# Decoding 64-bit weights through PSUM: the scaled high words move from an SBUF tile into the banks of the first MoE's output

## Chip, core and metric

One core of a Trainium2 chip runs the whole program. The metric is device time in microseconds (us): the time before is the median of three runs, 1158.89 us (1158.51 to 1161.87).

## What is computed

Attention with a top-32 mask over 4 x 8 heads of 576 tokens, then a dense feed-forward layer ("the first MoE", 2304 tokens, 512 to 2048 to 512, softplus between), then a layer of 8 experts with one expert per token. In short:

```
scores = scale * np.matmul(q, k.transpose(0, 1, 3, 2))
kth = np.partition(scores, -top_k, axis=-1)[..., -top_k:-top_k + 1]
attn = softmax(np.where(scores >= kth, scores, -1e9))
x = attn @ v            # as 2304 x 512
h = x @ w_in
x = (np.maximum(h, 0.0) + np.log1p(np.exp(-np.abs(h)))) @ w_out
...
h = np.maximum(xe @ w1[e], 0.0)
out[mask] = gate_w[mask, None] * (h @ w2[e])
```

`moe_w_in` and `moe_w_out` arrive as 64-bit floats, 8 bytes an element, and the kernel makes 32-bit floats of them itself. That decode is what the change touches.

## The kernel before

The program has two parts. Part one does attention, the decode and the first MoE, interleaved; part two does the experts.

**Attention** goes in 72 groups of two tiles of 128 query rows. For a group TensorE computes the scores (L365) into one PSUM tile, ScalarE copies them to SBUF (L373), VectorE finds the 32 largest of each row with maxima and replacements (L401 to L425) and makes the mask (L433 or L436), GpSimd applies the mask and splits the result into two 16-bit halves (L437, L442, L443), a DMA transposes them (L445), and three groups later TensorE multiplies with v (L460, L462). There is one PSUM tile for the scores, so the scores of the next group wait until VectorE has read it last, at L417.

**The decode** (`decode`, L196) takes 32 blocks of 128 x 512 weights: 16 of `w_in`, 16 of `w_out`, two ahead of the first group and then four behind each group in the program's text. For a block SyncE loads the 64-bit words (L198) into one of two tiles `w`; ScalarE scales the high word down (L204) into the SBUF tile `xr`; VectorE shifts that left by 3 bits, in place (L206), and joins it with the sign bit of the high word (L209), in place again; ScalarE scales the low word (L208), in place; GpSimd adds both as integers (L210). The tile `xr` has two buffers. A buffer is held from L204 until L210 has read it.

**The first MoE** goes in units of two tiles of 128 tokens, each of 16 steps (one per 128 columns of the hidden layer), 160 steps in all. A step has layer 1 (12 matmuls into `h`, L547; activations L551 to L555 on ScalarE; a sum into `g` on GpSimd, L556) and, two steps later, layer 2 (`layer2`, L570): one matmul per tile of tokens (L581, or L578 for the last units) that adds to the unit's two output tiles `y`. The pool `ps_y` of those tiles has two buffers, a PSUM bank each; `g` has four. Layer 1 can therefore run a few steps ahead of layer 2, and then has to wait for it.

**The order.** The order of instructions on each engine is fixed when the program is built: a list scheduler takes the program's text with priorities (attention ahead of decode and MoE) and its own estimate of times. Each engine then works through its list and waits at the front. A pool gives its buffers out in the order of the program's text: a tile that is asked for waits until the tile that held the buffer has been read last. In that text all 32 decodes stand ahead of the first unit's first layer-2 step.

```python
ps_y = pool("ps_y", 2, space=PSUM)
x2p = pool("x2p", X2B)
u.y = [ps_y.tile([128, DM], F32, name="y") for _ in u.tiles]
```

Of the kernel before, what the change touches and what calls it, by code (L numbers as in the profile page):

```python
# [8 lines left out]
F32 = mybir.dt.float32  # L9
F32R = mybir.dt.float32r  # L10
F16 = mybir.dt.float16
I32 = mybir.dt.int32
U32 = mybir.dt.uint32
AF = mybir.ActivationFunctionType
ALU = mybir.AluOpType
# [5 lines left out]
NT, DM, DFF = 2304, 512, 2048  # L21
# [11 lines left out]
ROWW = DM + 1  # L33
# [25 lines left out]
C = 512  # L59
# [103 lines left out]
def part_one(tc, ctx, q, k, v, w_in, w_out, const, ident, before, ones, iota_e, reg_e, wg,  # L163
             ohcum, done, early, table, rows, flags, sums, w_sums):
    nc = tc.nc
    late = []

    def pool(name, bufs, **kw):
        return ctx.enter_context(tc.tile_pool(name=name, bufs=bufs, **kw))
# [12 lines left out]
    x2p = pool("x2p", X2B)  # L182
# [3 lines left out]
    ps_y = pool("ps_y", 2, space=PSUM)  # L186
# [9 lines left out]
    def decode(src, kk, c0, dst):  # L196
        w = dec.tile([128, 2 * C], I32, name="w", bufs=DWB)
        nc.sync.dma_start(w, src[:, kk, 2 * c0:2 * (c0 + C)])  # L198
        w = w.rearrange("p (a b) -> p a b", b=2)
        hi, lo = w[:, :, 1], w[:, :, 0]  # L200
        a = x2p.tile([128, ROWW], F32, name="xr")[:, :C]


        nc.scalar.activation(a, hi.bitcast(F32), AF.Copy, scale=2.0 ** -111)  # L204
        u = a.bitcast(U32)
        nc.vector.tensor_scalar(u, u, 3, None, op0=ALU.logical_shift_left)  # L206

        nc.scalar.activation(lo, lo.bitcast(U32), AF.Copy, scale=2.0 ** -29)  # L208
        nc.vector.scalar_tensor_tensor(u, hi.bitcast(U32), 0x80000000, u, op0=ALU.bitwise_and, op1=ALU.bitwise_or)  # L209
        nc.gpsimd.tensor_tensor(out=dst.bitcast(I32), in0=a.bitcast(I32), in1=lo, op=ALU.add)  # L210

    def decode_w_in(kk, j):
        t = dec.tile([128, C], F32, name="t")
        decode(w_in_v, kk, j * C, t)
        nc.scalar.activation(w_in_s[:, kk, j, 1], t, AF.Abs, accum_out=w_sums[:, j, kk:kk + 1])
        nc.scalar.activation(w_in_s[:, kk, j, 0], t, AF.Copy)
        nc.gpsimd.tensor_tensor(out=w_in_s[:, kk, j, 1], in0=t, in1=w_in_s[:, kk, j, 0], op=ALU.subtract)
# [39 lines left out]
    for j in range(DFF // C):  # L257
        if flags is None:
            dec_q += [(decode, w_in_v, kk, j * C, w_in_f[:, kk, j]) for kk in range(KD)]
            dec_q += [(split_w_in, j)]  # L260
        else:
            dec_q += [(decode_w_in, kk, j) for kk in range(KD)]
        dec_q += [(decode, w_out_v, kk, c0, w_out_s[:, kk, c0:c0 + C])
                  for kk in range(j * C // 128, (j + 1) * C // 128) for c0 in range(0, DM, C)]
# [773 lines left out]
```

## Time and profile before

| | |
|---|---|
| median of three runs | 1158.89 us |
| the profiled execution | 1163.87 us, span 1162.2 us |
| busy, share of the span | TensorE 79%, VectorE 82%, ScalarE 69%, GpSimd 55% |
| chain that ended last | TensorE 34%, VectorE 27%, DMA 15%, issue 8%, ScalarE 7%, GpSimd 5% |
| granted TensorE clock, mean | 0.908 |

The shares are means over stages that differ: the decode runs in the first quarter, attention goes on for another 540 us beside the first MoE, and the experts follow. A stage has to be read by itself. The span is the time from the first to the last instruction of the profiled execution; its own time is 1.7 us more.

### The profile page before, as it was taken

The page shows a single profiled execution, that of the slowest core. Times are in us where ns is not written, and L with a number is a line of the kernel's source. Part 1 is how long each engine was busy: PE and PEld are TensorE (multiplying, and loading weights), DVE is VectorE, ACT ScalarE, POOL GpSimd, SP SyncE. Part 2 cuts the span into 40 slices and gives each one's busy share as a digit, 9 for nine tenths or more (in the row PEclk, how much of TensorE's full clock was granted, in tenths as well). Part 3 has the DMA queues.
Part 4 walks back from the last instruction along what each step waited for, and adds up shares of the span by engine and source line. Part 5 has one row for each costly group of instructions (what it writes and reads, how often), then busy time and mean ns, then how long its engine had stood idle before and what let it go on. Part 6 is the DMA issues. An engine that isn't in the chain of part 4 may idle for free.

```text
span 1162.2 us, 22614 instructions
## 1 busy us (share of the span) xinstructions
PE 922.5 (79%) x7146; PEld 662.0 (57%) x7146; DVE 948.7 (82%) x2980; ACT 803.0 (69%) x1898; POOL 640.4 (55%) x763
## 2 busy tenths in 40 slices
PE   1233377767799779888987898998998999999992
PEld 0112254434556455555655565565677889999981
DVE  4998999999787879888996898999654797777771
ACT  6676688877678759776886686776686755555561
POOL 3986889887576658556775665656532211211110
PEclk9995579768899899998998899998998999999997
DMA  8886778974858787335867443454520376676640
GB/s 198 195 199 132 166 170 193 197 164 90 108 91 144 119 117 157 74 71 83 158 132 108 82 80 72 71 72 79 176 55 16 96 217 218 208 255 212 232 176 25
DMA packets 295880, 157.18 MB, mean 135 GB/s; under 512 B 257524, under 2 KB 257652, under 8 KB 295732
## 3 DMA queue, kind: packets, MB, share of 16 engines
q1 hardware_dynamic: 292116, 145.73, 58.6%
q0 software_dynamic: 3616, 9.72, 2.5%
q8 instruction: 62, 1.02, 0.4%
q14 instruction: 86, 0.70, 0.3%
HBM read 77.89 MB, written 11.11 MB: 77 GB/s over the span
## 4 chain that ended last, share of the span: by engine, by line
PE 34%; DVE 27%; DMA 15%; issue 8%; ACT 7%; POOL 5%; SPq 2%; POOLq 0%; ACTq 0%; DVEq 0%
DMA pT<-p 8%; PE h L877 8%; PE y L890 8%; DVE mx L425 5%; PE h L547 5%; DVE wk L421 5%; PE y L581 4%; DVE e L433 2%; DVE mk L436 2%; PE y L578 2%; DVE wk L417 2%; DVE xr L209 2%; POOL p L443 2%; PE s L365 2%; PE m L460 2%
## 5 line engine op out<-in xcount | busy, mean ns | idle before, releaser
L581 PE MATMUL y<-w_out_s,g 128*128 128x512 f32 x480 | 247.7, 640 | 26.3 <-POOL g L556 26.3
L547 PE MATMUL h<-xT,w_in_s 128*128 128x256 f16 (+1 forms) x1920 | 240.3, 277 | 8.8 <-ACT g L553 5.3
L547 PEld LDWEIGHTS <-w_in_s 128*128 128x128 f16 x1920 | 178.2, 104 | 77.8 <-issue 51.1
L425 DVE MAX8 mx<-wk 128x8 f32<-128x144 f32 (+2 forms) x432 | 198.2, 493 | 0.1
L460 PE MATMUL m<-v,pT 128*128 128x65 f16 (+1 forms) x1440 | 105.9, 205 | 100.6 <-DMA pT<-p 81.1
L556 POOL TENSOR_TENSOR g<-g,sa 128x256 f32<-128x256 f32 (+1 forms) x160 | 117.5, 736 | 103.1 <-ACT sa L555 93.0
L443 POOL TENSOR_TENSOR p<-e,p 128x512 f16<-128x512 f32 x144 | 169.7, 1178 | 0.0
L365 PE MATMUL s<-kt,q 128*128 128x512 f16 (+7 forms) x640 | 104.2, 324 | 73.9 <-DVE wk L417 51.8
L460 PEld LDWEIGHTS <-pT 128*128 128x128 f16 (+1 forms) x1440 | 93.0, 109 | 121.6 <-DMA pT<-p 107.8
L421 DVE MATCH_REPLACE8 wk<-mx,wk 128x144 f32<-128x144 f32 (+1 forms) x432 | 144.3, 339 | 0.1
L441 ACT ACTIVATE p<-e 128x576 f16<-128x576 f32 x144 | 98.4, 683 | 64.8 <-POOL e L437 33.8
L581 PEld LDWEIGHTS y<-w_out_s,g 128*128 128x128 f32 x480 | 87.6, 204 | 94.7 <-issue 62.1
L437 POOL TENSOR_TENSOR e<-e,mk 128x576 f32<-128x576 f32 x84 | 110.9, 1322 | 50.0 <-DVE mk L436 40.4
L857 POOL DMA_INDIRECT out_dram<-ot,idx x19 | 19.9, 1045 | 177.7 <-DVE ot L856 174.9
L365 PEld LDWEIGHTS <-q 128*128 128x128 f16 (+1 forms) x640 | 46.8, 109 | 120.6 <-issue 43.2
L877 PEld LDWEIGHTS h<-xT,wf 128*128 128x128 f32 x864 | 111.9, 190 | 5.3 <-ACT wf L838 0.2
L877 PE MATMUL h<-xT,wf 128*128 128x256 f32 x864 | 114.0, 283 | 0.0
L890 PE MATMUL y<-wf,hT 128*128 128x512 f32 x432 | 112.6, 398 | 0.0
L414 ACT ACTIVATE e<-s,bias 128x576 f32<-128x576 f32 x144 | 105.6, 769 | 1.2 <-POOL p L443 0.4
L373 ACT ACTIVATE s<-s 128x1152 f32<-128x1152 f32 x72 | 81.0, 1125 | 10.5 <-PE s L365 10.1
L551 ACT ACTIVATE sa<-h 128x256 f32<-128x256 f32 (+1 forms) x160 | 57.2, 358 | 42.0 <-PE h L547 30.7
L890 PEld LDWEIGHTS y<-wf,hT 128*128 128x128 f32 x432 | 76.7, 189 | 13.2
(192 smaller groups left out, 1938.3 us busy)
## 6 DMA issues: line engine op xcount, KB each, us to landing
w1r<-in_moe_w_dram SPq DMA_DIRECT2D x20, 1024.0 KB, 5.3
w2r<-in_moe_w_dram SPq DMA_DIRECT2D x20, 1024.0 KB, 6.7
w<-in_moe_w_in_dram SPq DMA_DIRECT2D x16, 512.0 KB, 5.3
w<-in_moe_w_out_dram SPq DMA_DIRECT2D x16, 512.0 KB, 4.1
rows<-xr SPq DMA_DIRECT2D x37, 128.2 KB, 2.5
qn<-in_q_dram SPq DMA_DIRECT2D x16, 288.0 KB, 3.1
kn<-in_k_dram SPq DMA_DIRECT2D x16, 288.0 KB, 3.2
vn<-in_v_dram SPq DMA_DIRECT2D x16, 288.0 KB, 3.3
```

What stands on the lines that cost most here:

```text
L365: nc.tensor.matmul(ps[p0:p1, base + k0 * D:base + k1 * D], lhsT=lhs, rhs=kt[:, k0:k1, cs], start=first, stop=not first)
L414: nc.scalar.activation(e[i], s[i], AF.Exp, bias=bt[:, i], scale=SCORE if flags is not None else sc[i][:, 3:4])
L421: nc.vector.match_replace(out=to, in_to_replace=mx[:, i, 8 * j:8 * j + 8], in_values=src[i], imm_value=NEG)
L425: nc.vector.max(out=mx[:, i, 8 * j + 8:8 * j + 16], in_=src[i])
L437: nc.gpsimd.tensor_tensor(out=e[i], in0=e[i], in1=mk, op=ALU.mult)
L443: nc.gpsimd.tensor_tensor(out=p16[:, S + D:], in0=e[i][:, 0:S - D], in1=p16[:, 0:S - D], op=ALU.subtract)
L460: nc.tensor.matmul(o[:, h, 0:D + 1], lhsT=pT(r), rhs=v16[:, h, c, 0:D + 1], start=r == 0, stop=r == R - 1)
L547: nc.tensor.matmul(hps[:, :n], lhsT=w_in_s[:, c, j, p, o:o + 128], rhs=xT[:, 0:len(u.tiles), r, c, :], start=m == 0, stop=m == 3 * KD - 1)
L556: nc.gpsimd.tensor_tensor(out=g, in0=g, in1=a[:, :n], op=ALU.add)
L581: nc.tensor.matmul(u.y[i], lhsT=g[:, cs], rhs=w_out_s[:, f, :], start=f == 0, stop=f == KF - 1)
L877: nc.tensor.matmul(h, lhsT=w1f[:, a, c, :], rhs=xT[:, b, c, :], start=n == 0, stop=n == 3 * KD - 1)
L890: nc.tensor.matmul(y[i], lhsT=hT[g][:, a, i * 128:i * 128 + 128], rhs=w2f[:, b, :], start=g == 0 and n == 0, stop=g == KF2 - 1 and n == 2)
```

## The change

The scaled high word goes to a tile of `ps_y`, is shifted there, and is joined with the sign from there into a tile `xr`, which GpSimd then reads as before. Counts, shapes and loads stay as they are. All lines behind L201 move down by one in the changed file (L206 becomes L207, L581 becomes L582).

```diff
         hi, lo = w[:, :, 1], w[:, :, 0]
-        a = x2p.tile([128, ROWW], F32, name="xr")[:, :C]
+        a = ps_y.tile([128, DM], F32, name="y")
+        r = x2p.tile([128, ROWW], F32, name="xr")[:, :C].bitcast(U32)
 
 
         nc.scalar.activation(a, hi.bitcast(F32), AF.Copy, scale=2.0 ** -111)
         u = a.bitcast(U32)
         nc.vector.tensor_scalar(u, u, 3, None, op0=ALU.logical_shift_left)
 
         nc.scalar.activation(lo, lo.bitcast(U32), AF.Copy, scale=2.0 ** -29)
-        nc.vector.scalar_tensor_tensor(u, hi.bitcast(U32), 0x80000000, u, op0=ALU.bitwise_and, op1=ALU.bitwise_or)
-        nc.gpsimd.tensor_tensor(out=dst.bitcast(I32), in0=a.bitcast(I32), in1=lo, op=ALU.add)
+        nc.vector.scalar_tensor_tensor(r, hi.bitcast(U32), 0x80000000, u, op0=ALU.bitwise_and, op1=ALU.bitwise_or)
+        nc.gpsimd.tensor_tensor(out=dst.bitcast(I32), in0=r.bitcast(I32), in1=lo, op=ALU.add)
```

The order moves with it. First VectorE, one decode in the middle of the softmax of a group, with what each instruction waits for in brackets (the engine, or the DMA queue, whose count it waits on). Before:

```order
L206 TENSOR_SCALAR xr<-xr 128x512 [waits Activation_49,Pool_49]
L436 TENSOR_SCALAR mk<-s,mx 128x576 [waits DVE_49]
L403 TENSOR_TENSOR wk<-s,gt 128x2x144 [waits DVE_49]
L416 TENSOR_TENSOR wk<-s,gt 128x2x144
L417 TENSOR_TENSOR wk<-s 128x2x288
L484 TENSOR_SCALAR rc<-m 128x2 [waits PE_49]
L209 SCALAR_TENSOR_TENSOR xr<-w,xr 128x512 [waits DMAHW5_49,DVE_49]
```

In the change:

```order
L207 TENSOR_SCALAR y<-y 128x512 [waits Activation_49]
L437 TENSOR_SCALAR mk<-s,mx 128x576 [waits DVE_49,Pool_49]
L404 TENSOR_TENSOR wk<-s,gt 128x2x144 [waits DVE_49]
L417 TENSOR_TENSOR wk<-s,gt 128x2x144
L418 TENSOR_TENSOR wk<-s 128x2x288
L210 SCALAR_TENSOR_TENSOR xr<-w,y 128x512 [waits DMAHW4_49,DVE_49,Pool_49]
```

The shift now reads and writes `y`, and it is the join that waits for GpSimd, which must have read the `xr` of two decodes before.

Second, TensorE at the first layer-2 matmul of the first unit (`y`). Before, it stands behind the fourth layer-1 step, ahead of the scores of group 13 (groups are counted from 0), and waits for GpSimd's `g` alone:

```order
L547 MATMUL h<-xT,w_in_s 128x256
L547 LDWEIGHTS w_in_s
L547 MATMUL h<-xT,w_in_s 128x256
L581 MATMUL y<-w_out_s,g 128x512 [waits Pool_49]
L581 MATMUL y<-w_out_s,g 128x512
```

In the change it waits for VectorE, which must have done the last decode's join, and stands just ahead of the scores of group 20:

```order
L461 MATMUL m<-v_617,pT 128x65
L461 LDWEIGHTS pT
L461 MATMUL m<-v_617,pT 128x65
L582 MATMUL y<-w_out_s,g 128x512 [waits DVE_49]
L582 MATMUL y<-w_out_s,g 128x512 [waits Pool_49] x3
L461 LDWEIGHTS pT [waits DMAHW5_49]
```

Counted on TensorE's list, layer-1 steps and layer-2 steps of two matmuls that stand ahead of a group's scores:

| ahead of the scores of | before: layer 1, layer 2 | change: layer 1, layer 2 |
|---|---|---|
| group 20 | 13.8, 12 | 6, 2 |
| group 23 | 18, 15.5 | 16, 14 |
| group 71, the last: behind its last score matmul | 122.7, 112 | 120.0, 111 |

Third, GpSimd in the same place, where `g` (L556, L557 in the change) is a step of layer 1 and the two `p` pairs are one group of attention. Before:

```order
L437 TENSOR_TENSOR e<-e,mk 128x576
L442 TENSOR_TENSOR p_3106<-e,p_3106 128x64
L443 TENSOR_TENSOR p_3106<-e,p_3106 128x512
L442 TENSOR_TENSOR p_3112<-e,p_3112 128x64
L443 TENSOR_TENSOR p_3112<-e,p_3112 128x512
L556 TENSOR_TENSOR g<-g,sa 128x256
```

In the change:

```order
L557 TENSOR_TENSOR g<-g,sa 128x256 x3
L438 TENSOR_TENSOR e<-e,mk 128x576
L443 TENSOR_TENSOR p_3138<-e,p_3138 128x64
L444 TENSOR_TENSOR p_3138<-e,p_3138 128x512
L443 TENSOR_TENSOR p_3144<-e,p_3144 128x64
L444 TENSOR_TENSOR p_3144<-e,p_3144 128x512
L557 TENSOR_TENSOR g<-g,sa 128x256 x4
```

One or two steps per group have become three and four in a row: the steps that no longer stand ahead of group 20 stand here.

## Rows read from the trace of the kernel before

**Rows 1.** Stretches: busy us (instructions) of each engine, clock, DMA share, GB/s.
```profile
core 0: us, PE busy (x) PEld busy (x) DVE busy (x) ACT busy (x) POOL busy (x), PEclk, DMA share, GB/s
20.00:120.00 100.00, 31.00 (x272) 18.31 (x272) 93.18 (x269) 69.25 (x137) 78.36 (x75) 0.84 0.81 176
120.00:245.00 125.00, 82.74 (x642) 49.72 (x642) 124.69 (x339) 101.53 (x227) 112.61 (x110) 0.75 0.89 187
245.00:270.00 25.00, 16.33 (x134) 10.45 (x135) 24.21 (x70) 20.32 (x48) 20.60 (x21) 0.73 0.60 139
270.00:810.00 540.00, 466.12 (x3936) 305.56 (x3936) 468.88 (x1691) 394.19 (x975) 343.41 (x444) 0.93 0.59 100
810.00:912.00 102.00, 97.64 (x720) 73.62 (x718) 58.94 (x223) 76.03 (x238) 41.36 (x58) 0.93 0.30 77
```

**Rows 2.** Groups of VectorE's instructions, the decode's two: busy us, mean ns | idle before.
```profile
L209 DVE SCALAR_TENSOR_TENSOR xr<-w,xr 128x512 uint32<-128x512 uint32 x32 | 32.4, 1014 | 0.1
L206 DVE TENSOR_SCALAR xr<-xr 128x512 uint32<-128x512 uint32 x32 | 26.1, 815 | 8.7 <-ACT xr L204 8.7
```

**Rows 3.** The same two by source line: ns min/median/max, first and last start.
```profile
L206 DVE TENSOR_SCALAR xr<-xr x32: 402/855/1482, 10.5 to 260.4; 128x512 uint32<-128x512 uint32 x32
L209 DVE SCALAR_TENSOR_TENSOR xr<-w,xr x32: 672/975/1651, 10.9 to 261.4; 128x512 uint32<-128x512 uint32 x32
```

**Rows 4.** VectorE lines that read PSUM (`s`, `h`, `tp`, `y`), by source line.
```profile
L401 DVE TENSOR_TENSOR s<-s x72: 435/452/467, 19.6 to 801.1; 128x288 f32<-128x288 f32 x72
L882 DVE SCALAR_TENSOR_TENSOR hT<-h,hT x72: 405/425/426, 918.4 to 1126.2; 128x256 fp32r<-128x256 f32 x72
L849 DVE TENSOR_TENSOR xT<-tp,xT x19: 680/683/694, 847.8 to 1121.5; 128x512 fp32r<-128x512 f32 x19
L856 DVE TENSOR_SCALAR ot<-y,xg x19: 729/743/750, 941.0 to 1142.1; 128x512 f32<-128x512 f32 x19
```

**Rows 5.** Who waited for whom, 20 to 270 us: total, times, longest.
```profile
DVE xr L206 <- ACT xr L204: 6.9, 4, 2.8
ACT xr L204 <- DMA w<-in_moe_w_in_dram: 13.4, 6, 3.9
```

**Rows 6.** Timeline: GpSimd's sum of the eleventh decode, VectorE's join of the thirteenth.
```profile
109.17 1.47 POOL L210 TENSOR_TENSOR t<-xr,w 128x512 int32<-128x512 int32 x1
...
118.26 1.15 DVE L209 SCALAR_TENSOR_TENSOR xr<-w,xr 128x512 uint32<-128x512 uint32 x1
```

**Rows 7.** First softmax instruction of groups 19, 20, 23 and 25 (VectorE's timeline).
```profile
245.96 0.45 DVE L401 TENSOR_TENSOR s<-s 128x288 f32<-128x288 f32 x1
...
252.35 0.46 DVE L401 TENSOR_TENSOR s<-s 128x288 f32<-128x288 f32 x1
...
286.88 0.45 DVE L401 TENSOR_TENSOR s<-s 128x288 f32<-128x288 f32 x1
...
306.52 0.45 DVE L401 TENSOR_TENSOR s<-s 128x288 f32<-128x288 f32 x1
```

**Rows 8.** Layer 2 of the first units, by source line (a 32-bit matmul makes two records).
```profile
L581 PE MATMUL y<-w_out_s,g x480: 592/592/1222, 157.6 to 829.4; 128*128 128x512 f32 x160
```

**Rows 9.** TensorE's timeline, 230 to 295 us: steps of both layers, scores, products with v.
```profile
237.83 5.04 PE L581 MATMUL y<-w_out_s,g 128*128 128x512 f32 x8
...
255.33 5.28 PE L547 MATMUL h<-xT,w_in_s 128*128 128x256 f16 x24 [2.67 <-ACT g L553]
...
263.23 3.70 PE L581 MATMUL y<-w_out_s,g 128*128 128x512 f32 x8 [0.49 <-POOL g L556]
...
282.01 0.19 PE L460 MATMUL m<-v,pT 128*128 128x65 f16 x1
...
282.87 1.15 PE L365 MATMUL s<-kt,q 128*128 128x512 f16 x8
...
285.21 1.47 PE L547 MATMUL h<-xT,w_in_s 128*128 128x256 f16 x12
```

## The prediction

> **What bounds the kernel now.** I read it by stretches first, because the shares over the span mix four stages. The stretches [rows 1] show where VectorE is the limit: from 120 to 245 us it is busy 124.69 of 125, from 245 to 270 24.21 of 25, and from 20 to 120 93.18 of 100. That is the decode, whose instructions start between 10.5 and 261.4 us [rows 3], beside the first 21 groups of attention. In the same 125 us GpSimd is busy 112.61 and the DMA engines 0.89: both are close behind. From 270 to 810 us nobody is full (TensorE 466 of 540, VectorE 469), and from 810 to 912 TensorE is busy 97.64 of 102: what is left of the first MoE then runs at TensorE's pace.
>
> So an instruction that leaves VectorE before 270 us can shorten the program, and a matmul that is moved behind 810 us lengthens it. The change does both.
>
> **The change, step by step.** *VectorE's two instructions.* The 32 shifts take 815 ns in the mean and the 32 joins 1014 [rows 2]. Their ranges are wide: the shift 402 to 1482, the join 672 to 1651 [rows 3], for one shape each. A VectorE instruction that takes one operand from PSUM has no such range: L401, which runs beside the same GpSimd from 19.6 us on, takes 435 to 467 in 72 executions [rows 4]. I read the wide ranges as waits for GpSimd in the access to SBUF. In the change the shift touches PSUM alone and the join takes one operand from there, so both should have a narrow time. Its size: L401 takes 452 ns for 288 columns, L882 425 for 256, L849 683 for 512 [rows 4], some 1.03 ns a column between the last two; 512 columns then cost about 685 ns, for the shift as for the join. The shift loses its fast case (402) and gains its slow ones. Per decode: 815 + 1014 - 2 x 685 = 459 ns, times 32 is **14.7 us**. By L856, a scale from PSUM at 743 [rows 4], it would be 343 ns and 11.0 us; were both as fast as their shortest (402 and 672) 24 us. I take 685, because L401 is the one that reads and writes PSUM as the shift will.
>
> The Trainium skill says in "SBUF — State Buffer", section "Who interferes with whom", that a VectorE instruction with two SBUF inputs, or in a two-port mode, and a GpSimd instruction exclude each other for the whole of it, and that one with at most one SBUF input outside those modes doesn't contend. The ranges of [rows 3, 4] agree.
>
> *How much of it arrives.* VectorE has 0.3 us to spare in 125, so nearly all should. But the DMA share of 0.89 and GpSimd's 0.90 [rows 1] leave room for a tenth, and the decode is itself a loop: a load goes into the tile `w` that GpSimd has just left, ScalarE waited 13.4 us for such loads and VectorE 6.9 for ScalarE in turn [rows 5]. A VectorE that is 6% faster will meet these more often. I take **10 us**, between 5 (a third) and 14.7 (all).
>
> *The new wait of the join.* It waits for GpSimd to have read `xr` two decodes before. At the tightest place of the trace GpSimd ended that sum at 109.17 + 1.47 = 110.64 us, and the join two decodes later started at 118.26 [rows 6]: 7.6 us in hand. Nothing; if GpSimd were that late, VectorE's whole list would stand. ScalarE's write to PSUM and the earlier return of its buffer change nothing here, as ScalarE is busy 101.53 of 125 [rows 1].
>
> *The tiles of layer 2.* This is the price. The unit's two output tiles come behind 32 decode tiles in the same two buffers. Before, layer 2 began at 157.6 us [rows 8]; now its first matmul waits for the last join, in group 19, and `g`'s four buffers stop layer 1 after six steps. By the counted order TensorE has 6 layer-1 and 2 layer-2 steps ahead of the scores of group 20, where it had 13.8 and 12, and must do 10 and 12 between there and the scores of group 23, where it did 4.2 and 3.5.
>
> At its faster pace a layer-2 step takes 3.70 / 2 = 1.85 us and a layer-1 step 1.47, overlapped with the next by some 0.15; two products with v take 282.87 - 282.01 = 0.86 and scores 1.15 [rows 9]. The stretch then needs 12 x 1.72 + 10 x 1.31 + 4 x 0.43 + 3 x 1.0 = 38.4 us, and the two layer-2 steps that stand ahead of group 20's scores another 3.4: 41.8. VectorE went from group 20 to 23 in 286.88 - 252.35 = 34.5 us [rows 7], of which two decodes, 3.7, will be gone: 30.8. TensorE is late by 11; some 2 us of that VectorE has in hand, since scores are made ahead. I take **9 us lost**. Low end 3, if steps slip into gaps of later groups; high end 20, at the slower pace (5.04 and 5.28 us for two steps [rows 9]), which TensorE had here when it had been idle before: 12 x 2.52 + 10 x 2.64 + 8 = 65 us would cost 34, but it won't stay at it while it is full.
>
> *The end of part one.* Behind the last scores TensorE has 160 - 120.0 = 40.0 layer-1 steps left where it had 37.3, and one layer-2 step more. In the stretch 810 to 912 it is full [rows 1], so they count whole: 2.7 x 1.31 + 1.72 = **5.3 us lost**; 2 to 8 for the bounds, as the last units' layer 2 has another form.
>
> *Hidden at no cost:* fewer steps of the first MoE before 245 us free ScalarE and GpSimd for the decode, which VectorE bounds; part two is untouched.
>
> **The sum.** -10 + 9 + 5 = **+4 us** on the profiled span of 1162.2, so 1166. That execution took 1163.87 in all, 5.0 over the median of 1158.89. Carried to the median: **1163 us**. A difference under 0.3%, 3.5 us, can't be told from none here.
>
> **Rivals.** *Faster: the gain arrives and the catching up is absorbed.* For it: TensorE has 74 idle us between 270 and 810 [rows 1], and the trace shows VectorE going from group 23 to 25 in 19.6 us, more than its own work. Then 13 us are gained, 3 lost in catching up and 5 at the end: -5, 1154 us. It decides if TensorE is less than 5 us late at group 23. Against it: the list is fixed, and the two-step lag is still there at the last group. 0.24.
>
> *No change: gain and loss cancel,* 8 gained, 4 + 5 lost or 12 gained, 7 + 5 lost: 1156 to 1162. 0.28.
>
> *Slower by much: the decode does not get faster.* If the DMA (0.89) binds as soon as VectorE is faster, 5 us arrive, and with 12 and 6 lost it is +13, 1172. 0.12 of the 0.48 for slower.
>
> *The change does not do what it says.* If the wide range of the join isn't GpSimd's doing, the join stays at 1014 and the shift becomes 685: 0.13 x 32 = 4.2 us gained, 14 lost, 1169. Against it, the narrow range of L401. 0.06, also within slower. The Trainium skill speaks against the shift itself: "VectorE: DVE Perf Modes", section "Why PSUM operands drop a tier", says that a 32-bit source in PSUM runs at half the rate that a single SBUF source can have. The fast case of 402 ns against 452 for 288 PSUM columns agrees [rows 3, 4]; by that rule alone the shifts would cost 32 x 0.28 = 9 us more VectorE time, an estimate that leaves the waits out.
>
> **How the numbers follow.** The forecast, slower by about 4, has 0.30; with the two slower rivals 0.48. The range takes the gain at 14 with losses of 6 (-8) and the gain at 5 with losses of 18 (+13): **1151 to 1172**. Within the forecast itself it is 1162 to 1167. Chances: faster 0.24, same 0.28, slower 0.48.
>
> **What would show it.** Shift and join at about 685 ns with hardly a range; the last join some 10 us earlier than 261.4; layer 2 starting there and not at 157.6; groups 20 to 23 taking 38 us or more, with VectorE idle for ScalarE's copy of the scores (L374) and TensorE without a gap; the stretch behind the last group a few us longer. It is wrong if group 23 begins 8 us or more earlier than 286.88, or if shift or join still spread to 1.5 us, or if VectorE waits at the join for GpSimd.

## The result and the profile after

The change takes 1173.45 us (median of four runs, 1170.50 to 1177.29) against 1160.38 for the kernel before beside it: ratio 1.0119, 95% interval 1.0079 to 1.0160. It is slower, as forecast, but by 13 us and not by 4, and the time lies 1.5 us above the range. The profiled execution took 1170.5 us, its span is 1168.8. In a second comparison (six runs) the ratio was 1.0122 [1.0075, 1.0168], and its profile agrees with the first to within 1.5 us at every mark used below.

VectorE's two instructions first, by source line (ns min/median/max, first and last start), with GpSimd's sum and the first layer-2 matmul:

```profile
L207 DVE TENSOR_SCALAR y<-y x32: 668/686/700, 10.2 to 238.8; 128x512 uint32<-128x512 uint32 x32
L210 DVE SCALAR_TENSOR_TENSOR xr<-w,y x32: 658/670/686, 10.9 to 239.9; 128x512 uint32<-128x512 uint32 x32
L211 POOL TENSOR_TENSOR t<-xr,w x16: 1277/1284/1347, 11.8 to 217.8; 128x512 int32<-128x512 int32 x16
L582 PE MATMUL y<-w_out_s,g x480: 592/592/1222, 234.2 to 837.8; 128*128 128x512 f32 x160
```

Against [rows 3] the wide ranges are gone: the shift had 402 to 1482 and has 668 to 700, the join had 672 to 1651 and has 658 to 686. GpSimd's sum, at 1277 to 1347, has lost its spread too. The last join starts at 239.9 and not 261.4. But layer 2 [rows 8] starts at 234.2 and not 157.6.

The prediction inferred from the ranges that shift and join wait for GpSimd. The trace of the kernel before shows the wait itself; here are a sum of GpSimd and the join that [rows 6] has beside it:

```profile
117.39 1.47 POOL L210 TENSOR_TENSOR t<-xr,w 128x512 int32<-128x512 int32 x1
118.26 1.15 DVE L209 SCALAR_TENSOR_TENSOR xr<-w,xr 128x512 uint32<-128x512 uint32 x1
```

The sum ends at 118.86, the join 0.55 us later. Of the 32 joins 19 start while an instruction of GpSimd has more than 0.25 us to go, and each of them ends 0.55 us after that instruction; the other 13 take 672 to 787 ns. Of the 32 shifts 18 start like that; 17 end 0.28 to 0.29 us after GpSimd's instruction and one 0.33, and the other 14 take 402 to 527 ns. In the change 21 shifts and 17 joins start beside such an instruction and take no longer than the rest.

The stretches of [rows 1], after the change:

```profile
20.00:120.00 100.00, 32.73 (x286) 19.16 (x286) 94.65 (x284) 74.11 (x147) 80.55 (x81) 1.00 0.83 192
120.00:245.00 125.00, 60.44 (x553) 39.50 (x553) 119.23 (x361) 99.09 (x214) 104.49 (x107) 0.63 0.91 193
245.00:270.00 25.00, 24.57 (x147) 15.42 (x148) 20.36 (x60) 16.05 (x39) 16.58 (x21) 1.00 0.39 80
270.00:810.00 540.00, 478.54 (x3981) 311.83 (x3979) 457.16 (x1654) 395.85 (x989) 338.26 (x440) 0.94 0.59 99
810.00:912.00 102.00, 94.09 (x688) 70.63 (x687) 54.16 (x211) 69.19 (x214) 35.45 (x53) 0.95 0.25 70
```

From 120 to 245 us TensorE was busy 82.74 and is busy 60.44: 22 us of its work have left this stretch. From 245 to 270 it is the full engine, 24.57 of 25, and VectorE, which had 24.21, has 20.36. The bound has changed hands there.

Next comes VectorE's timeline, the first softmax instruction of groups 19, 20, 21, 23, 25 and 71. For the kernel before, [rows 7] has groups 19, 20, 23 and 25; here are 21 and 71:

```profile
268.73 0.45 DVE L401 TENSOR_TENSOR s<-s 128x288 f32<-128x288 f32 x1
...
801.07 0.44 DVE L401 TENSOR_TENSOR s<-s 128x288 f32<-128x288 f32 x1
```

After the change:

```profile
232.43 0.47 DVE L402 TENSOR_TENSOR s<-s 128x288 f32<-128x288 f32 x1 [0.27 <-ACT s L374]
...
244.35 0.44 DVE L402 TENSOR_TENSOR s<-s 128x288 f32<-128x288 f32 x1
...
260.86 0.47 DVE L402 TENSOR_TENSOR s<-s 128x288 f32<-128x288 f32 x1 [4.14 <-ACT s L374]
...
283.62 0.47 DVE L402 TENSOR_TENSOR s<-s 128x288 f32<-128x288 f32 x1 [1.34 <-ACT s L374]
...
300.90 0.46 DVE L402 TENSOR_TENSOR s<-s 128x288 f32<-128x288 f32 x1
...
800.95 0.46 DVE L402 TENSOR_TENSOR s<-s 128x288 f32<-128x288 f32 x1
```

The program is ahead by 13.5 us at group 19, by 8.0 at group 20, by 7.9 at group 21, by 3.3 at group 23, by 5.6 at group 25 and by 0.1 at group 71. TensorE's timeline shows the first place where the lead goes:

```profile
234.24 5.33 PE L582 MATMUL y<-w_out_s,g 128*128 128x512 f32 x8
...
239.83 1.15 PE L366 MATMUL s<-kt,q 128*128 128x512 f16 x8
240.82 3.65 PE L582 MATMUL y<-w_out_s,g 128*128 128x512 f32 x8
...
245.07 1.47 PE L548 MATMUL h<-xT,w_in_s 128*128 128x256 f16 x12
246.38 1.88 PE L582 MATMUL y<-w_out_s,g 128*128 128x512 f32 x4
```

Two layer-2 steps at the slower pace stand ahead of the scores of group 20, and from there the steps follow each other almost without a gap. From group 20 to group 23 TensorE is busy 38.74 of 39.27 us, VectorE 29.55:

```profile
244.35:283.62 39.27, 38.74 (x277) 24.55 (x276) 29.55 (x92) 26.47 (x66) 24.78 (x31) 1.00 0.34 69
```

VectorE's waits (us in total, times, longest) from 270 to 810 us, after the change:

```profile
DVE rc L485 <- PE m L461: 37.3, 13, 9.3
DVE s L402 <- ACT s L374: 22.5, 11, 5.7
```

and in the kernel before:

```profile
DVE rc L484 <- PE m L460: 36.5, 14, 5.7
DVE s L401 <- ACT s L373: 9.8, 7, 4.8
```

The wait for the scores' copy, which is TensorE coming late with the scores, has grown by 12.7 us (in the second pair of profiles from 9.3 to 23.3). In the same stretch the lead falls from 7.9 us, at group 21, to 0.1.

### The profile page after: what moved, and what is told of

It reads as the page before. It is cut to its first block, busy times and chain, and to the rows that moved or that the text cites. A ratio compares the mean times of both kernels' runs of the same rounds, so it can differ in the third digit from the quotient of the medians.

```text
span 1168.8 us, 22587 instructions
## 1 busy us (share of the span) xinstructions
PE 925.2 (79%) x7146; PEld 665.4 (57%) x7146; DVE 928.6 (79%) x2980; ACT 801.9 (69%) x1898; POOL 622.4 (53%) x763
## 5 line engine op out<-in xcount | busy, mean ns | idle before, releaser
L582 PE MATMUL y<-w_out_s,g 128*128 128x512 f32 x480 | 245.5, 633 | 17.5 <-POOL g L557 17.5
L548 PE MATMUL h<-xT,w_in_s 128*128 128x256 f16 (+1 forms) x1920 | 234.7, 272 | 13.5 <-ACT g L554 10.1
L461 PE MATMUL m<-v,pT 128*128 128x65 f16 (+1 forms) x1440 | 117.4, 208 | 122.4 <-DMA pT<-p 91.5
L461 PEld LDWEIGHTS <-pT 128*128 128x128 f16 (+1 forms) x1440 | 98.9, 110 | 135.6 <-DMA pT<-p 118.3
L557 POOL TENSOR_TENSOR g<-g,sa 128x256 f32<-128x256 f32 (+1 forms) x160 | 112.1, 703 | 119.1 <-ACT sa L556 102.2
L366 PE MATMUL s<-kt,q 128*128 128x512 f16 (+7 forms) x640 | 114.8, 333 | 58.9 <-DVE wk L418 34.8
L422 DVE MATCH_REPLACE8 wk<-mx,wk 128x144 f32<-128x144 f32 (+1 forms) x432 | 144.4, 339 | 0.1
L582 PEld LDWEIGHTS y<-w_out_s,g 128*128 128x128 f32 x480 | 85.8, 201 | 80.1 <-issue 57.2
L438 POOL TENSOR_TENSOR e<-e,mk 128x576 f32<-128x576 f32 x84 | 108.2, 1290 | 41.0 <-DVE mk L437 18.9
L366 PEld LDWEIGHTS <-q 128*128 128x128 f16 (+1 forms) x640 | 50.2, 112 | 105.9 <-issue 34.5
L374 ACT ACTIVATE s<-s 128x1152 f32<-128x1152 f32 x72 | 80.8, 1123 | 19.7 <-PE s L366 19.5
L463 PE MATMUL m<-v,pT 128*128 128x64 f16 (+1 forms) x800 | 86.8, 207 | 0.0
```

Source lines behind the costliest of these rows:

```text
L366: nc.tensor.matmul(ps[p0:p1, base + k0 * D:base + k1 * D], lhsT=lhs, rhs=kt[:, k0:k1, cs], start=first, stop=not first)
L422: nc.vector.match_replace(out=to, in_to_replace=mx[:, i, 8 * j:8 * j + 8], in_values=src[i], imm_value=NEG)
L438: nc.gpsimd.tensor_tensor(out=e[i], in0=e[i], in1=mk, op=ALU.mult)
L461: nc.tensor.matmul(o[:, h, 0:D + 1], lhsT=pT(r), rhs=v16[:, h, c, 0:D + 1], start=r == 0, stop=r == R - 1)
L548: nc.tensor.matmul(hps[:, :n], lhsT=w_in_s[:, c, j, p, o:o + 128], rhs=xT[:, 0:len(u.tiles), r, c, :], start=m == 0, stop=m == 3 * KD - 1)
L557: nc.gpsimd.tensor_tensor(out=g, in0=g, in1=a[:, :n], op=ALU.add)
```

## The experiments

Theory A: the decode does get faster, and layer 2 pays for it, because its two tiles stand behind the last decodes in the same two banks and TensorE has no room to make up the work that this pushes back. The rivals are those of the expectations; a letter holds within its batch. A number in brackets behind a ratio is its 95% interval. The 0.473 us that a decode spares VectorE is 815 + 1014 - 686 - 670 ns. Counts that the expectations place "ahead of group 71" (112 and 101 for the kernel before) are by the traces those ahead of group 65's scores; ahead of group 71's stand 122.7 and 112.

The kernels from "Which of the two instructions" on ran on another chip than the four ahead of them. There the kernel before took 1164.89 and 1167.34 us (medians of two batches) and not 1159.32, and no trace of it was kept. So the table of traces at the end compares across chips; each ratio compares kernels on the same one.

**The change in part, from the front.** One line decides by the number of the decode (counted as the program is written); the same edit with other conditions serves below.

```diff
-        a = ps_y.tile([128, DM], F32, name="y")
         r = x2p.tile([128, ROWW], F32, name="xr")[:, :C].bitcast(U32)
+        count[0] += 1
+        a = ps_y.tile([128, DM], F32, name="y") if count[0] <= 18 else r.bitcast(F32)
```

> The first 18 decodes go through PSUM as in the change, the last 14 through SBUF as before, so no output tile of the first MoE waits for a decode behind the eighteenth. On TensorE's list 13.5 layer-1 and 12 layer-2 steps stand ahead of group 20's scores (before 13.8 and 12, change 6 and 2), and 124.0 and 114 ahead of the end of the last scores (before 122.7 and 112). Theory A, the wait for the two banks is the loss: 18 x 0.46 = 8 us of VectorE's time are gained, little is lost, the kernel is 4 to 9 us faster than before (ratio 0.992 to 0.997), and layer 2 begins near 155 us. Rival B, moving decode work into PSUM costs by itself (the faster decode runs into DMA and GpSimd, or the scheduler's new order is bad wherever the tile lies): about 18/32 of the change's loss, 4 to 8 us slower than before.

Measured: 1150.21 us, ratio 0.9922 [0.9893, 0.9951]. The eighteenth join starts at 144.4 us and layer 2 at 146.9 (155 was expected). With the banks free again before layer 2 wants them, the same edit is a gain of 9 us and beats both kernels.

**The price alone.** The condition is `count[0] > 30`: only the last two decodes go through PSUM.

> Only the last 2 of the 32 decodes go through PSUM; 30 are as before. The first MoE's output tiles still come behind the last decode: on TensorE's list 6 layer-1 steps and no layer-2 step stand ahead of group 20's scores, and 120.0 and 111 ahead of the end of the last scores, as in the change. Theory A: the whole price without the gain, so slower than the change: 14 to 22 us slower than before (ratio 1.012 to 1.019), with the last decode's join near 260 us. Rival B: only 2/32 of the change's loss, within 2 us of before.

Measured: 1180.95 us, ratio 1.0192 [1.0154, 1.0229]. Two decodes of 32, and the program loses more than with all of them. Layer 2 by source line, and the stretch from group 20 to group 23:

```profile
L585 PE MATMUL y<-w_out_s,g x480: 592/592/1222, 253.9 to 847.9; 128*128 128x512 f32 x160
```

```profile
252.94:301.80 48.86, 47.21 (x291) 28.40 (x292) 32.58 (x97) 29.24 (x69) 26.51 (x33) 0.95 0.36 71
```

TensorE is busy 47.21 of 48.86 us, VectorE 32.58. In the kernel before the same three groups were VectorE's, with TensorE a quarter idle:

```profile
252.35:286.88 34.53, 25.87 (x191) 16.23 (x190) 33.89 (x103) 27.38 (x64) 26.61 (x30) 0.77 0.56 114
```

This run prices the wait: 21.6 us (1180.95 less 1159.32, the kernel before of that batch) and some 0.9 that the two decodes gain. The change in the same batch took 1170.12, so its other 30 decodes are worth 10.8 us while the wait is being paid.

**The change and the kernel before once more,** beside these two.

> The change once more, for a second profiled execution and more times. Theory A: 8 to 14 us slower than before; shift and join again at 0.67 to 0.70 us with no range; group 20 begins some 8 us earlier than in the first profile of before, and that lead is gone by the last group. If the first profile of before was simply a slow execution, the last group of this one begins no earlier than 800 us.

> The kernel before once more, for a second profile of it. Its first profiled execution took 1163.87 us, 3.5 more than the median of 1160.38, so this one should show where executions of one kernel differ: I expect the same time to group 21 within 3 us, and the last group to begin 3 to 5 us earlier than 801.1 us.

Measured: 1170.12 us and 1160.77; both profiles are used in the table below. The change repeats itself: its group 20 begins 6.9 us ahead of the first profile of before (8 expected), its group 71 only 1.6. The last group of the kernel before began at 800.9 and not, as I expected, 3 to 5 us earlier than 801.1. What made its first profiled execution longer lies behind that group: from there to the last layer-1 activation the two took 109.0 and 106.1 us, at a granted clock of 0.92 and 0.95 (the change, twice: 0.96).

**Which of the two instructions.** In the first 18 decodes only the shift (first diff) or only the join (second diff) has an operand in PSUM.

```diff
-        nc.vector.tensor_scalar(u, u, 3, None, op0=ALU.logical_shift_left)
+        nc.vector.tensor_scalar(r, u, 3, None, op0=ALU.logical_shift_left)
...
-        nc.vector.scalar_tensor_tensor(r, hi.bitcast(U32), 0x80000000, u, op0=ALU.bitwise_and, op1=ALU.bitwise_or)
+        nc.vector.scalar_tensor_tensor(r, hi.bitcast(U32), 0x80000000, r, op0=ALU.bitwise_and, op1=ALU.bitwise_or)
```

```diff
-        nc.scalar.activation(a, hi.bitcast(F32), AF.Copy, scale=2.0 ** -111)
+        nc.scalar.activation(r.bitcast(F32), hi.bitcast(F32), AF.Copy, scale=2.0 ** -111)
         u = a.bitcast(U32)
-        nc.vector.tensor_scalar(u, u, 3, None, op0=ALU.logical_shift_left)
+        nc.vector.tensor_scalar(u, r, 3, None, op0=ALU.logical_shift_left)
```

> In the first 18 decodes alone the scaled high words go to PSUM and the shift reads them there, but writes the SBUF tile; the join has two SBUF operands as in the kernel before. Theory A (TensorE's list counts): VectorE is spared 18 x (0.815 - 0.686) = 2.3 us, of which two thirds arrive, 1.6; TensorE's list is the one of the version with 18 decodes (13.5 and 12 steps ahead of group 20, 113 and 103 ahead of group 71, against 112 and 101 before), which at 1.31 and 1.72 us a step is worth 1.3 + 3.4 = 4.7 us behind group 71. Sum -6: 1153, ratio 0.995. Theory B (only VectorE's time counts, the list doesn't): -1.6, 1157.7, ratio 0.9986. Theory C (the shift still waits for GpSimd, since it writes SBUF): its range stays wide and nothing is spared; the list alone, 1154.5.

> In the first 18 decodes alone the scaled high words go to the SBUF tile, the shift writes them to PSUM, and the join has one operand from there. Join at 670 ns with hardly a range; shift unknown (one SBUF operand: 400 if it no longer waits, 815 if it does). VectorE is spared at least 18 x (1.014 - 0.670) = 6.2 us, two thirds 4.2. The list: ahead of group 71 110.7 and 100 steps (before 112 and 101), but behind the last scores as many left as before. Theory A1 (steps are counted ahead of group 71): + 1.7 + 1.7 = 3.4, sum -0.8, 1158.5, ratio 0.9993. Theory A2 (they are counted at the last scores, as the prediction did) and theory B (VectorE's time alone): -4.2, 1155, ratio 0.9964; were the shift at 400 as well, 7 us more on VectorE and 5 more on the time in either.

Measured: shift alone 0.9969 [0.9904, 1.0034], join alone 0.9943 [0.9912, 0.9973]. The first is inconclusive as a time (theories A and B both lie in its interval); its trace settles theory C, as the shift's range is gone. Shift and join by source line, of the kernel with the shift alone:

```profile
L210 DVE TENSOR_SCALAR xr<-y x18: 665/678/692, 9.1 to 144.4; 128x512 uint32<-128x512 uint32 x18
L210 DVE TENSOR_SCALAR xr<-xr x14: 408/698/1427, 149.0 to 263.2; 128x512 uint32<-128x512 uint32 x14
L213 DVE SCALAR_TENSOR_TENSOR xr<-w,xr x32: 667/807/1685, 9.8 to 265.1; 128x512 uint32<-128x512 uint32 x32
```

and of the kernel with the join alone:

```profile
L210 DVE TENSOR_SCALAR y<-xr x18: 667/682/697, 9.4 to 143.2; 128x512 uint32<-128x512 uint32 x18
L213 DVE SCALAR_TENSOR_TENSOR xr<-w,y x18: 664/674/689, 10.1 to 144.2; 128x512 uint32<-128x512 uint32 x18
L213 DVE SCALAR_TENSOR_TENSOR xr<-w,xr x14: 668/920/1681, 149.1 to 258.7; 128x512 uint32<-128x512 uint32 x14
```

One operand in PSUM is enough, on either side: the shift takes 678 from PSUM to SBUF, 682 from SBUF to PSUM, 686 within PSUM, all within 35 ns. For the shift into PSUM I had expected 400 or 815: it is neither. The forms with SBUF alone keep their range in the same programs. For the join alone, theory A1 (0.9993) is out: the interval ends at 0.9973. A2 and B fit. A1 rested on the count ahead of group 65; ahead of group 71 this kernel (122.8 and 112 steps) and the one before (122.7 and 112) are level, so it says nothing on where steps must be counted.

**How late may layer 2 start?** Conditions `count[0] <= 24`, `<= 28` and, in the last batch, `<= 22`.

> The first 24 decodes through PSUM, the last 8 as before. VectorE is spared 24 x 0.473 = 11.4 us, two thirds 7.7. Layer 2 starts some 4 groups later than before but stands at 14 and 10 steps ahead of group 20 (before 13.8 and 12) and at 111.3 and 101 ahead of group 71 (112 and 101). Theory A: 0.7 x 1.31 = 0.9 lost at the end, hardly anything at group 20: -6.8, 1152.5, ratio 0.994. Theory B (the decode's saving alone; 18 decodes gave 9): -12, 1147, ratio 0.9895. Theory C (any wait of layer 2 for the decode's banks costs the 20 us of the version with only the last two): 1171, ratio 1.010.

> The first 28 decodes through PSUM, the last 4 as before. VectorE is spared 28 x 0.473 = 13.2 us, two thirds 9.0. Ahead of group 20 stand 11 and 8 steps (before 13.8 and 12; with all 32 it is 6 and 2), ahead of group 71 110.1 and 100 (112 and 101). Theory A: to be caught up 2.8 x 1.31 + 4 x 1.72 = 10.6 us of TensorE; with all 32 27.4 us cost about 10 by group 71, so 3.7 here; behind group 71 1.9 x 1.31 + 1.72 = 4.2. Sum -1.1: 1158, ratio 0.999. Theory B (the decode's saving alone): -14, 1145, ratio 0.988. Theory C (any wait of layer 2 costs 20): 1170, ratio 1.009.

Measured: first 24 0.9883 [0.9836, 0.9930], first 28 0.9940 [0.9902, 0.9979]. Theory C, that any wait costs, is out. Theory A's own gains were too small on both, and with 28 theory B (0.988) is out as well: some 7 of its 13.2 us arrive. Where layer 2 isn't far behind, the decode's saving arrives in full and not by two thirds: with 24 it is 24 x 0.473 = 11.4 us, and measured were 13.6 by the ratio and 10.4 between the medians (13 by both in the repeat below; first 22, below, is the exception). With 28, layer 2 by source line and TensorE from 200 to 300 us:

```profile
L585 PE MATMUL y<-w_out_s,g x480: 592/592/1220, 206.8 to 820.7; 128*128 128x512 f32 x160
```

```profile
200.00:300.00 100.00, 88.82 (x688) 55.03 (x688) 98.64 (x313) 79.10 (x185) 74.38 (x83) 0.96 0.64 135
```

and the same 100 us in the change:

```profile
200.00:300.00 100.00, 77.39 (x583) 48.47 (x584) 89.07 (x284) 76.05 (x173) 70.59 (x79) 0.81 0.58 122
```

Layer 2 starts 49 us later than before in the kernel with 28, and VectorE is still full: TensorE makes it up. From group 20 to group 23 it just can, at a granted clock of 1.00, busy 28.00 of 29.20 us while VectorE is busy 29.06:

```profile
245.80:275.00 29.20, 28.00 (x222) 17.92 (x220) 29.06 (x95) 24.80 (x59) 21.56 (x27) 1.00 0.51 102
```

Starting 27 us later again, in the change, VectorE stands for 11 of the 100 us.

**With room on TensorE.** Two of layer 1's three passes are left out, in the kernel before and in the change alike, so the wait for the banks stays and TensorE has time.

```diff
-            for p, r in ((0, 0), (0, 1), (1, 0)):
+            for p, r in ((0, 0),):
...
-                                 start=m == 0, stop=m == 3 * KD - 1)
+                                 start=m == 0, stop=m == KD - 1)
```

> The kernel before with one of layer 1's three passes (the high halves' product alone; the two that mix high and low halves are left out): a step has 4 matmuls for 12, some 0.9 us less, 140 us less TensorE work in all. It is the base for the next kernel. Both theories: part one no longer ends at TensorE's pace, so 20 to 60 us shorter than the kernel before, ratio 0.95 to 0.98.

> The change with the same two passes of layer 1 left out. Layer 2 waits for the last join exactly as in the change (6 and 0 steps ahead of group 20, against 13.5 and 12 in the base), but TensorE has slack, and its list has as many steps ahead of group 71 as the base's (114.8 and 104 against 115 and 104). Theory A (the price is TensorE's missing slack): catching up costs 0 to 5 us, nothing at the end, 11 to 14 gained: 6 to 14 us faster than the kernel with one pass without the change, ratio between the two 0.988 to 0.995. Theory D (the wait for the two banks costs by itself, whatever TensorE's load): as in the change, 10 to 14 us slower than it, 1.009 to 1.012.

Measured: 1153.17 us without the change (0.9897 [0.9849, 0.9945], less of a gain than I expected: the last layer-1 activation starts at 896.0, 11 to 14 us earlier than in the kernel before), 1144.07 with it (0.9832 [0.9775, 0.9890]). The change now gains 9.1 us, ratio 0.992 between the two medians, and the slowest of its four runs (1151.43) is faster than the fastest of the other four (1152.91). Theory D is out: whatever the wait for the banks may cost by itself, it is not the 20 us that it costs without the room. Little is left of the price: from group 20 to group 23 VectorE was busy 30.80 of 33.00 us. Layer 2 by source line, with the change:

```profile
L582 PE MATMUL y<-w_out_s,g x480: 592/592/1222, 243.5 to 788.2; 128*128 128x512 f32 x160
```

and without:

```profile
L581 PE MATMUL y<-w_out_s,g x480: 592/592/1222, 155.9 to 795.5; 128*128 128x512 f32 x160
```

Layer 2 of these units starts 88 us later and yet its last matmul starts 7 us earlier.

**The best cut once more, and one beside it.**

> The first 24 decodes through PSUM once more, beside the next one. The gain in full (24 x 0.473 = 11.4) less 1 at the end, or what was measured, 13.6: ratio 0.988 to 0.991. If the first measurement was a slow base's doing: 0.994.

> The first 22 decodes through PSUM. Ahead of group 20 stand 14 and 12 steps (before 13.8 and 12), ahead of group 71 113.1 and 103 (112 and 101): layer 2 starts later and nothing is behind. By VectorE's time in full: 22 x 0.473 = 10.4, ratio 0.991. If the steps ahead of group 71 count as well, 1.1 x 1.31 + 2 x 1.72 = 4.9 us more, ratio 0.987. If only two thirds of the gain arrive and the list doesn't count, 0.994.

Measured: first 24 0.9886 [0.9835, 0.9937], as before; first 22 1.0014 [0.9984, 1.0044], no gain at all. That is a miss for every theory of mine. Its first softmax instructions of groups 25, 30 and 71:

```profile
298.74 0.46 DVE L405 TENSOR_TENSOR s<-s 128x288 f32<-128x288 f32 x1
...
362.46 0.47 DVE L405 TENSOR_TENSOR s<-s 128x288 f32<-128x288 f32 x1 [1.04 <-ACT s L377]
...
804.77 0.47 DVE L405 TENSOR_TENSOR s<-s 128x288 f32<-128x288 f32 x1 [3.85 <-ACT s L377]
```

It is 7.8 us ahead of the first profile of before at group 25, like its neighbours, 2.4 ahead at group 30 (before: 364.9) and 3.7 behind at group 71. From 270 to 810 us VectorE waited 24.3 us for the scores' copy, about as long as in the change (22.5), although as many steps as before or more stood ahead of the scores of groups 20 and 71. This profiled execution, at 1159.40, was the fastest of ten with a median of 1166.51.

**All of them side by side.** Steps on TensorE's list ahead of group 20's scores, and from the traces the starts of groups and the start of the last layer-1 activation (L551 before), in us:

| PSUM decodes | steps | 19 | 20 | 23 | 25 | 71 | last activation | span |
|---|---|---|---|---|---|---|---|---|
| none (before) | 13.8, 12 | 246.0 | 252.3 | 286.9 | 306.5 | 801.1 | 910.0 | 1162.2 |
| none, again | 13.8, 12 | 245.5 | 251.8 | 287.1 | 306.7 | 800.9 | 907.0 | 1159.0 |
| all 32 (the change) | 6, 2 | 232.4 | 244.4 | 283.6 | 300.9 | 801.0 | 916.5 | 1168.8 |
| all 32, again | 6, 2 | 233.5 | 245.5 | 284.8 | 302.1 | 799.5 | 915.6 | 1168.2 |
| first 18 | 13.5, 12 | 233.6 | 244.2 | 279.7 | 297.4 | 794.7 | 894.4 | 1146.3 |
| first 22 | 14, 12 | 234.8 | 246.4 | 279.4 | 298.7 | 804.8 | 905.6 | 1157.7 |
| first 24 | 14, 10 | 237.2 | 248.0 | 279.6 | 297.9 | 787.4 | 899.8 | 1152.9 |
| first 24, again | 14, 10 | 237.4 | 248.3 | 281.2 | 299.5 | 788.6 | 899.0 | 1153.5 |
| first 28 | 11, 8 | 236.5 | 245.8 | 275.0 | 293.5 | 790.0 | 901.4 | 1154.2 |
| last 2 | 6, 0 | 243.5 | 252.9 | 301.8 | 319.1 | 811.1 | 926.3 | 1178.7 |
| first 18, shift alone | 13.5, 12 | 235.4 | 247.1 | 282.4 | 300.1 | 806.0 | 907.0 | 1159.3 |
| first 18, join alone | 13.5, 12 | 231.5 | 241.1 | 276.4 | 295.1 | 793.7 | 902.7 | 1155.8 |

At group 25 the table is in order: every cut that moves both instructions and leaves eight or more layer-2 steps ahead of group 20 leads by 7 to 13 us, the change by 4.6 to 5.6, the last two alone trail by 12 to 13. From group 25 to group 71 the programs take 494.5 and 494.2 (before, twice), 489.5 and 489.2 (first 24, twice), 500.1 and 497.4 (the change, twice), 492.0 (last two), 496.5 (first 28), 497.3 (first 18), 506.0 (first 22) and 505.9 us (first 18, shift alone). A program repeats its own number to within 3 us, and the programs differ by up to 17, with the same work in this stretch but for a few steps. First 18 and its shift alone even have the same steps ahead of groups 20 and 71, and differ by 8.6. I read this as each program's own order of instructions; no run separates that from anything else. What the change loses behind group 25 may be in part of this kind.

## Why the prediction was right and wrong

Lead and loss at the marks of the prediction, from the two pairs of profiles in the table (before and change, then both again):

| step | predicted | measured |
|---|---|---|
| gain of the decode, at group 19 | 10 (5 to 14.7) | 13.5, 12.0 |
| catching up, groups 19 to 23 | -9 (-3 to -20) | -10.3, -9.7 |
| groups 23 to 71 | 0 | -3.1, -0.8 |
| end of part one, group 71 to the last activation | -5.3 (-2 to -8) | -6.6, -10.0 |
| sum | -4 | -6.5, -8.6 |

*VectorE's instructions: right.* 685 ns each was forecast; 686 and 670 were measured, with hardly a range. In the groups of VectorE's instructions the two fell from the 26.1 and 32.4 us of [rows 2] to 21.9 and 21.4: 15.2 us, against 14.7 forecast. The trace agrees with the Trainium skill's rule of the prediction ("SBUF — State Buffer", section "Who interferes with whom"): the waits for GpSimd's instructions, above, are gone where an operand is in PSUM, and the part kernels agree form by form. (The 1.03 ns a column that the prediction takes from "the last two" lines is from L401 and L849; the last two give 1.01. The 685 stays.) The lost fast case of the shift was real and was outweighed.

*How much arrives: too low.* I took two thirds. At group 19 12 to 13.5 us had arrived, and in the kernels with the first 18 and 24 decodes all of it. DMA did rise, from 0.89 to 0.91, but VectorE waited no longer for the scaled words than before (8.2 us at L207, 8.7 at L206).

*The wait of the join: right.* VectorE stood idle for 0.1 us in all ahead of its 32 joins, and none of that is put down to GpSimd.

*The tiles of layer 2: right in kind and in size.* Layer 2 started at 234.2, the three groups took 39.27 us ("38 us or more"), and VectorE waited for L374. Group 23 began 3.3 us early where the sum gave 1. The part kernels show why it was not simply a wait. What first 28 pushed back (2.8 x 1.31 + 4 x 1.72 = 10.6 us) just fitted between groups 20 and 23, where TensorE was busy 28.00 us and VectorE 29.06. The change pushed back 7.8 x 1.31 + 10 x 1.72 = 27.4 us, and TensorE was busy 38.74 us where VectorE was 29.55: 9.2 us too much, against the 9 forecast. The idle time of TensorE in the kernel before, 34.53 - 25.87 = 8.7 us, would not have given the limit, since its granted clock was 0.77 in that stretch and 1.00 in the other two.

*Behind group 23: the step that failed, by its size.* The prediction put nothing at groups 23 to 71 and "2.7 x 1.31 + 1.72 = 5.3 us lost" at the end of part one. Measured were 3.1 + 6.6 = 9.7 us and 0.8 + 10.0 = 10.8, about twice as much. With the catching up the price came to 20.0 and 20.6 us, where the sum had 14.3. The 5.3 was counted at the last score matmul; the trace counts at the moment at which VectorE begins group 71. What TensorE still had to do then, before (by source line, from 801.07 us on):

```profile
L547 PE MATMUL h<-xT,w_in_s x432: 217/272/421, 802.6 to 909.7; 128*128 128x256 f16 x80, 128*128 128x128 f16 x64
L581 PE MATMUL y<-w_out_s,g x27: 592/592/1222, 800.7 to 829.4; 128*128 128x512 f32 x27
```

and after (from 800.95 us on):

```profile
L548 PE MATMUL h<-xT,w_in_s x476: 217/272/418, 800.7 to 916.2; 128*128 128x256 f16 x95, 128*128 128x128 f16 x64
L582 PE MATMUL y<-w_out_s,g x36: 592/592/1057, 802.9 to 837.8; 128*128 128x512 f32 x36
```

That is (476 - 432) / 12 = 3.7 layer-1 steps and (36 - 27) / 4 = 2.25 layer-2 steps (a step makes four records): 3.7 x 1.31 + 2.25 x 1.72 = 8.7 us, where this pair shows 6.6. In the second pair the count gives 2.9 and 2 steps, 7.3 us, and the traces show 10.0. So the count gives the end to within 3 us, which is also what two executions of the kernel before differ by in this stretch. Before, the last score matmul had started 4.9 us before VectorE began group 71, and TensorE had gone on; in the change it was 2.2 us. The steps left at that moment also order most of the other kernels: with the first 18 or 22 decodes 34 to 35 layer-1 and 4 layer-2 steps were left and the last activation came 99.7 and 100.8 us later; with the last two 38 and 9, and 115.2. First 24, with as many left as the kernel before (36 and 7 to 7.5), took 112.4 and 110.3, some 1 to 6 us more than that. Why groups 23 to 71 cost 3.1 and 0.8 us stays open.

*The range: too short at its upper end,* because the price was bounded at 12 + 6 = 18 us. The change paid 20.0 and 20.6 by its traces, the kernel with the last two decodes alone 21.6 in its time. Gain and price were both larger than forecast, so the direction held and the difference did not.

*From the profile to the median: the larger part of the miss.* The forecast of 1163 is 10.5 us below the measured 1173.45. Only 2.8 of that is in the span (1166 forecast, 1168.8 measured). The other 7.7 come from the step "carried to the median": it took off 3 us from span to median, because the profiled execution of the kernel before had been a long one, while the median of the change lies 4.7 above its profiled span (in the second comparison 1.9).

*What stays open.* By the profiles the change loses 6.6 and 9.2 us (spans), by the medians 13.1 and 10.8. Its ten runs lie at 1167.7 to 1170.9 (six, both profiled ones among them) and 1176.0 to 1179.8 (four). No trace shows one of the four, so what they do in those 6 us wasn't seen.

*The rivals.* "The decode does not get faster" and "the change does not do what it says" fell with the trace. "Gain and loss cancel" is out by the interval. "The decode does not get faster" had come nearest to the measured time, with 1172, but by a DMA limit that the trace doesn't show: that was luck. "The catching up is absorbed" is not this kernel, but it is what happens up to group 25 with the first 28 decodes and, but for some 2 us, with one pass of layer 1.

## What to carry to other kernels

A scratch tile that borrows a pool of PSUM buffers also takes its place in that pool's order: ask who wants the buffers next and what stands behind that request, before counting what the borrower gains. Work that is pushed back on an engine was nearly free here as long as the engine could do it in the time that the other engine needed in that stretch anyway (28.00 us of TensorE beside 29.06 of VectorE), and cost the excess beyond that (38.74 beside 29.55). So compare the two in that stretch, at the clock that the engine will have there, and not over the span. Where an edit also reorders the program, compare at the first mark behind the edit as well as at the end: first 22 gained 8 us at group 25 like its neighbours and had lost them at group 71, for a reason that no run shows. And carry a forecast from a profiled execution to the median only with several executions of both kernels at hand.

## What was not expected of the hardware

A 128 x 512 shift costs the same with PSUM as source, as target or as both (678, 682 and 686 ns), so one end in PSUM is enough to take the shift's spread away; for the join only an input there was tried. GpSimd's sum became steadier as well: before, the two groups of L210 took 1391 and 1372 ns in the mean (up to 1802), and now, as L211, 1290 and 1287. Before, 11 of the 32 took over 1.4 us: eight started while a shift was running, one while a join was, and two while L433 was. In the change none does.
